# Whole 128 blocks in a padded MLP, and table work moved between engines, in a fused adaLN, long-convolution and MLP kernel

## The chip, the cores and the metric

The kernel runs on one core of a Trainium2 chip. The time is device microseconds of one execution; the number given for a kernel is the median of several executions. The engines of the core work side by side and meet through semaphores: PE (TensorE, matmuls; its weight loads are listed apart as PEld), DVE (VectorE), ACT (ScalarE), POOL (GpSimd) and SP (SyncE, which here only issues DMAs).

## The reference

A sequence of 2048 tokens of width 640 goes through a layernorm with scale and shift, a long convolution by FFT (a state-space mixer), a second modulated layernorm, and an MLP block. Cut to what matters:

```python
def _A_ref(q, k, v, shift_k, ssm_k, ssm_D):     # S = 2048, D = 640
    k_shift = sum of 4 shifted copies of k, each times a column of shift_k
    kv = k_shift * v
    y = irfft(rfft(pad(kv, 2*S)) * rfft(pad(ssm_k, 2*S)))[:S]
    return q * (y + kv * ssm_D)

def _B_ref(x, w1, w2, w3, w4):                  # F = 1728
    h = gelu(layernorm(x) @ w1)                 # 640 -> 640
    hs = (quarters of h, shifted by 1, -1, 2, -2 tokens) @ w2
    x1 = x + hs
    return x1 + gelu(layernorm(x1) @ w3) @ w4   # 640 -> 1728 -> 640

sa, ca, ga, sb, cb, gb = silu(c) @ w_mod
h = layernorm(x) * (1 + ca) + sa
x = x + ga * _A_ref(h, k, v, shift_k, ssm_k, ssm_D)
h = layernorm(x) * (1 + cb) + sb
out = x + gb * _B_ref(h, w1, w2, w3, w4)
```

All tensors are bf16. The inner width 1728 is 13 blocks of 128 and one of 64.

## The kernel before

**How work is ordered.** The kernel writes down tasks (`add(engine, cost, function, r=, w=, prio=)`), each with an engine, an estimated cost in us, the regions it reads and writes, and a priority (smaller goes first). A planner (`Planner.run`, L90) then simulates the five engines with these costs: an engine that comes free takes, among the tasks whose inputs are ready, the one with the smallest priority. The order that comes out is fixed: each engine executes its instructions strictly in that order, and semaphores make it wait where the data is not there. So a cost or a priority changed in one place can move instructions of other tasks, and an engine that stands at one instruction holds everything behind it in its queue.

**The convolution.** The FFT of length 4096 is done as two stages of matmuls against tables of sines and cosines, and its inverse likewise. The tables are made in the kernel at its start: POOL writes integer ramps (`iota`), DVE turns them into angles (`angles`, L316: a multiply-add at L323, a bitwise and for the modulus at L324), and ACT takes the sine (`sin_to`, L328; the instruction is at L331).

- `F1bd` is the block-diagonal table of stage 1: eight Sins of 32 rows by 32 columns into a zeroed tile (L284).
- `Gs` (in region RG) is the table of stage 2, in four blocks `kb`: from one ramp of 512 columns, eight DVE pairs and 16 Sins of 128x512, four of which write the same cosine a second time.
- `EA` and `EB` are small tables of the first inverse stage.
- `Hs` (in region RH) is the table of the last inverse stage, in four blocks `nb`: one ramp, eight DVE pairs, eight Sins of 128x512. Its integer scratch lies in region RK.

First the state-space kernel `ssm_k` is loaded (region Ra), turned by five DVE transposes (`to_slots`, L386, each after a one-column add, L442) and transformed (stage 1 at L399, stage 2 at L418, PSUM evacuated by ACT at L229 or DVE at L231). Meanwhile k is transposed on PE (L461), shifted by matmuls with diagonal weights (`diagw`, made by a POOL select at L350; L474) and multiplied with v on DVE (L480); the product goes through the same stages. The modulation vectors come from `w_mod` (loads at L497, matmuls at L507, called mod pieces here), which need the Silu of c at L378; that Silu stands behind the last Sin of the H table. The input x is loaded at L543 into region Ra when the second stage 1 has read it. The first inverse stage (`inverse1`: a DMA at L603 that swaps halves, two DVE products at L608 and L610, matmuls at L619 and L620) is followed by the last one (`inverse2`, L648).

**The MLP block.** Eight groups `g` of 256 tokens pass through DVE chains and layernorms, whose small statistics are computed on POOL (`ln_finish`, L685 to L694, and `ln1_fin`, L575 to L578). SP turns normalized tokens by DMA transposes (L734, called hT here, and L839). Then `mm_w1` (L764, L774), `mm_w2` (L819), `mm_w3` (L854, gelu at L859, L861 and L862) and `mm_w4` (L877). In `mm_w3` the stationary operand is a block of w3 (128 rows by 128 columns, the last one 64 columns) and 256 tokens move; five matmuls add up one block, 14 blocks make 70 matmuls a group. In `mm_w4` the stationary operand is a block of the gelu's output (128 features by 128 tokens, the last one 64 features) and 320 output columns move; 14 matmuls for each half of a tile of 128 tokens make 56 a group. w3 and w4 are loaded by SP (L900 to L902) over the region T01 once inverse2 has read it.

Of the kernel before, what the change touches and what calls it, by code (L numbers as in the profile page):

```python
# [8 lines left out]
BF = mybir.dt.bfloat16  # L9
F32 = mybir.dt.float32  # L10
# [6 lines left out]
P = 128  # L17
# [4 lines left out]
PI_LO = 3.1415925  # L22
LFFT = 4096
# [134 lines left out]
def kernel(  # L158
# [125 lines left out]
    add("POOL", 0.3, lambda e: nc.gpsimd.memset(F1bd[:], 0.0), w=[("F1", 0, 1)], prio=-2)  # L284
    add("POOL", 0.6, lambda e: make_identity(nc, ident), w=[("modB", 5, 6)], prio=5)

    def f(e):
        nc.vector.tensor_single_scalar(pci[:, 0:1], pidx[:], 31, ALU.bitwise_and)
        nc.vector.tensor_single_scalar(pci[:, 1:2], pidx[:], 63, ALU.bitwise_and)
        nc.vector.tensor_copy(s32[:], pci[:, 0:1])  # L290
        nc.vector.tensor_scalar(s32o[:], pci[:, 0:1], 2.0, 1.0, ALU.mult, ALU.add)
        nc.vector.tensor_copy(s64[:], pci[:, 1:2])
    add("DVE", 0.7, f, r=[("pidx", 0, 1)], w=[("scol", 0, 1)], prio=-2)

    gcol = mem.tile([P, 2, 4], F32, name="gcol")
    hcol = mem.tile([P, 2, 4], F32, name="hcol")
    ci = mem.tile([P, 4], I32, name="ci")

    def f(e):
        nc.gpsimd.iota(ci[:], pattern=[[16, 4]], base=0, channel_multiplier=0)  # L300
    add("POOL", 0.2, f, w=[("ci", 0, 1)], prio=-3)

    def f(e):
        for col, s_ in ((gcol, s64), (hcol, s32o)):
            nc.vector.tensor_scalar(col[:, 0, :], ci[:], s_[:], None, ALU.mult)
            nc.vector.tensor_scalar(col[:, 1, :], ci[:], s_[:], 2048.0, ALU.mult, ALU.add)
    add("DVE", 0.5, f, r=[("ci", 0, 1), ("scol", 0, 1)], w=[("cols", 0, 1)], prio=-1)
    tmp = {"R3": R3[:].bitcast(I32), "RK": RK[:].bitcast(I32)}

    def itab(reg, o, n, pattern, base, prio):  # L310
        ti = tmp[reg][:, o:o + n]
        add("POOL", 0.2 + 0.0012 * n, lambda e: nc.gpsimd.iota(ti, pattern=pattern, base=base, channel_multiplier=0),
            w=[(reg, 2 * o, 2 * o + 2 * n)], prio=prio)
        return ti, (reg, 2 * o, 2 * o + 2 * n)

    def angles(it, reg, o, s_col, cs_col, ss_col, q, prio):  # L316
        ti, tk = it
        n = ti.shape[1]
        ms, ma = (tmp[reg][:, o + n * i:o + n * (i + 1)] for i in range(2))
        keys = [(reg, 2 * o + 2 * n * i, 2 * o + 2 * n * (i + 1)) for i in range(2)]  # L320
        for m_, k_, col in ((ms, keys[0], ss_col), (ma, keys[1], cs_col)):
            def f(e, m_=m_, col=col):
                nc.vector.tensor_scalar(m_, ti, s_col, col, ALU.mult, ALU.add)  # L323
                nc.vector.tensor_single_scalar(m_, m_, q - 1, ALU.bitwise_and)  # L324
            add("DVE", 0.2 + 0.0013 * n, f, r=[tk, ("cols", 0, 1), ("scol", 0, 1)], w=[k_], prio=prio)
        return ms, ma, keys
# [6 lines left out]

    it = itab("R3", 4608, 32, [[2, 32]], 1, -2)
    ms, ma, ky = angles(it, "R3", 4640, s32[:], 32.0, 0.0, 128, -1)
    for q in range(4):
        sl = slice(32 * q, 32 * q + 32)
        sin_to(F1bd[sl, q, 0, :], ma[sl, :], 128, 32, ky[1], ("F1", 0, 1, "f"), -1)
        sin_to(F1bd[sl, q, 1, :], ms[sl, :], 128, 32, ky[0], ("F1", 0, 1, "f"), -1, True)
    it = itab("R3", 0, 512, [[2, 8], [128, 64]], 1, -1)  # L340
    for kb in range(4):
        ms, ma, ky = angles(it, "R3", 512 + 1024 * kb, s64[:], gcol[:, 1, kb:kb + 1], gcol[:, 0, kb:kb + 1], 8192, -1)
# [6 lines left out]
        sin_to(Gs[:, k2s, 1, 1, :], ma3, 8192, 512, ky[1], wk, 0)  # L349
# [5 lines left out]
    it = itab("RK", 1536, 64, [[1, 64]], 0, 8)  # L355
    ms, ma, ky = angles(it, "RK", 1600, s64[:], 16.0, 0.0, 64, 30)
# [11 lines left out]
    it = itab("RK", 0, 512, [[1, 16], [64, 32]], 0, 8)  # L368
    for nb in range(4):
        ms, ma, ky = angles(it, "RK", 512, s32o[:], hcol[:, 1, nb:nb + 1], hcol[:, 0, nb:nb + 1], 8192, 30)  # L370
        n1s = slice(16 * nb, 16 * nb + 16)
        wk = ("RH", 1024 * nb, 1024 * nb + 1024, "h")
        sin_to(Hs[:, n1s, 0, :], ma.rearrange("p (a b) -> p a b", a=16), 8192, 512, ky[1], wk, 30)
        sin_to(Hs[:, n1s, 1, :], ms.rearrange("p (a b) -> p a b", a=16), 8192, 512, ky[0], wk, 30, True)
# [285 lines left out]
    w3_sb = T0[:, 0:ND * F].rearrange("p (b n) -> p b n", b=ND)  # L660
# [180 lines left out]
    def mm_w3(g, prio):  # L841
        xT, xTk = xnT[g % 3]
        gk3 = ("R5", 10240 + 3584 * (g % 2), 10240 + 3584 * (g % 2) + 3584, ("g3", g))
        for f0 in range(0, NF, 4):
# [3 lines left out]
            def f(e, ps=ps, f0=f0, fn=fn):  # L848
                pt = pst(ps, [P, 4, 256], name="ps_w3")
                for fl in range(fn):  # L850
                    fb = f0 + fl
                    fw = min(P, F - fb * P)
                    for b in range(ND):
                        nc.tensor.matmul(pt[:fw, fl, :], lhsT=w3_sb[:, b, fb * P:fb * P + fw], rhs=xT[:, b, :], start=(b == 0), stop=(b == ND - 1))  # L854
# [114 lines left out]
```

## Time and profile before

| what | value |
|---|---|
| median of three runs | 369.92 us (368.13 to 370.08) |
| profiled execution | 368.94 us |
| its span, first to last instruction | 367.2 us |
| mean granted TensorE clock | 0.916 |
| PE busy | 290.1 us, 79% |
| PEld busy | 213.8 us, 58% |
| DVE busy | 234.7 us, 64% |
| ACT busy | 226.8 us, 62% |
| POOL busy | 80.1 us, 22% |

Busy time is the time in which an engine executes instructions; a share of the whole span hides that the stages have different limits, so stages are read one at a time. The chain of waits is followed back from the last instruction: at each step to what released it, or to the instruction before it on its engine. In the chain, "x56" means 56 instructions of one line in one piece. In a row of a timeline or a group, the line number is that of the kernel, what is written stands left of the arrow, and shapes are partitions by elements; for a matmul or a weight load, "64*128" are the active rows and columns of the array.

### The profile page before, as it was taken

Reading aid. Unit: us, or ns where it says so; the run is one execution under the profiler, and the core shown is the slowest. Engines: PE = TensorE matmul, PEld = TensorE weight load, DVE = VectorE, ACT = ScalarE, POOL = GpSimd, SP = SyncE. Lnnn points to the kernel's source line nnn. Section 1 sums busy time; section 2 is a strip of 40 time slices with the busy share of each in tenths; the row PEclk is TensorE's granted clock in tenths of the full one; section 3 lists DMA queues with packets and bytes.
Section 4 is the critical chain, followed back from the end, with each engine's and each line's share of the span. In section 5 each row is a group of like instructions: output and inputs, shape, how many; then the busy total and the mean of one; then the engine's idle time right before and its main releaser. Section 6 shows DMA issues by size and latency. Waiting matters only on the chain.

```text
span 367.2 us, 7656 instructions
## 1 busy us (share of the span) xinstructions
PE 290.1 (79%) x3086; PEld 213.8 (58%) x3092; DVE 234.7 (64%) x436; ACT 226.8 (62%) x362; POOL 80.1 (22%) x201
## 2 busy tenths in 40 slices
PE   0459789899834787501686999999999999999993
PEld 0336445577524776401554887786776776768672
DVE  8999999889089899988789786532313031211313
ACT  6959886679905588887789897693471412213020
POOL 8300000000020001485587573341130000000000
PEclk9989999999985799555868999999999999999997
DMA  7999404085962580079012505205010212101001
GB/s 217 339 199 234 142 0 116 2 266 108 215 206 67 133 203 4 4 290 267 3 36 54 91 15 108 61 0 83 26 38 20 54 29 45 38 10 29 18 21 36
DMA packets 49060, 35.08 MB, mean 96 GB/s; under 512 B 35008, under 2 KB 45952, under 8 KB 49024
## 3 DMA queue, kind: packets, MB, share of 16 engines
q1 hardware_dynamic: 47984, 30.39, 34.8%
q0 software_dynamic: 1040, 4.20, 3.4%
q8 instruction: 24, 0.39, 0.4%
q14 instruction: 12, 0.10, 0.1%
HBM read 18.85 MB, written 2.62 MB: 58 GB/s over the span
## 4 chain that ended last, share of the span: by engine, by line
PE 55%; DVE 25%; DMA 8%; ACT 4%; issue 3%; POOL 3%; SPq 1%; DVEq 0%; POOLq 0%; ACTq 0%
PE ps_w L877 18%; PE ps_w L854 18%; PE ps_w L819 6%; PE ps_w L764 5%; DMA Ra<-in_A_q_dram 4%; DVE ln_st L569 3%; DVE Rb L386 3%; DVE R L480 2%; DVE Rb L610 2%; DVE Ra L386 2%; ACT T L229 2%; PE ps_ksh L474 2%; DMA R<-RK 2%; PE ps_s L399 2%; DVE T L231 2%
## 5 line engine op out<-in xcount | busy, mean ns | idle before, releaser
L854 PE MATMUL ps_w<-R,T 128*128 128x256 bf16 (+1 forms) x560 | 66.3, 277 | 2.6 <-DMA R<-RH 2.6
L883 DVE TENSOR_TENSOR T<-ps_w,R 128x640 bf16<-128x640 f32 x16 | 13.2, 825 | 86.3 <-PE ps_w L877 86.3
L877 PE MATMUL ps_w<-T,R 128*128 128x320 bf16 x448 | 68.1, 300 | 0.0
L859 ACT ACTIVATE R<-ps_w 128x1024 bf16<-128x1024 f32 x24 | 24.5, 1022 | 61.7 <-PE ps_w L854 61.6
L854 PEld LDWEIGHTS <-T 128*128 128x128 bf16 (+1 forms) x560 | 54.5, 100 | 13.2 <-issue 6.0
L877 PEld LDWEIGHTS <-R 128*128 128x128 bf16 x448 | 41.7, 97 | 25.6 <-issue 8.4
L229 ACT CAST R<-ps_s 128x640 bf16<-128x640 f32 x49 | 31.4, 744 | 3.2 <-PE ps_s L418 3.2
L764 PE MATMUL ps_w<-R,RG 128*128 128x256 bf16 x160 | 20.4, 287 | 16.3 <-DMA R<-RK 16.3
L619 PE MATMUL ps_i<-EA,Rb 128*128 128x128 bf16 x160 | 23.2, 243 | 11.4 <-DVE Rb L608 11.4
L819 PE MATMUL ps_w<-RG,R 128*128 128x320 bf16 x160 | 25.7, 317 | 5.5 <-ACT R L780 4.1
L699 ACT ACTIVATE RG<-R 128x640 bf16<-128x640 bf16 x32 | 23.5, 736 | 9.9 <-DVE R L827 7.3
L229 ACT CAST T<-ps_s 128x1024 bf16<-128x1024 f32 x25 | 23.7, 1020 | 7.3 <-PE ps_s L399 7.3
L399 PE MATMUL ps_s<-F1bd,Rb 128*128 128x256 bf16 x80 | 13.3, 337 | 18.7 <-DVE Ra L442 14.3
L764 PEld LDWEIGHTS <-RG 128*128 128x128 bf16 x160 | 16.4, 103 | 19.7 <-issue 16.6
L418 PE MATMUL ps_s<-T,RG 64*128 64x160 bf16 x512 | 24.4, 230 | 2.8 <-ACT R L229 0.5
L620 PE MATMUL ps_i<-EB,Rb 128*128 128x128 bf16 x160 | 23.0, 243 | 3.7 <-DVE Rb L610 3.7
L229 ACT CAST T<-ps_i 128x1024 bf16<-128x1024 f32 x20 | 19.6, 1014 | 10.1 <-PE ps_i L620 6.5
L619 PEld LDWEIGHTS <-Rb 128*128 128x128 bf16 x160 | 17.8, 111 | 11.9 <-DVE Rb L608 11.9
L418 PEld LDWEIGHTS <-RG 64*128 64x128 bf16 x512 | 18.1, 94 | 10.9 <-issue 10.2
L819 PEld LDWEIGHTS <-R 128*128 128x128 bf16 x160 | 15.9, 103 | 13.6 <-ACT R L780 4.8
L399 PEld LDWEIGHTS <-Rb 128*128 128x128 bf16 x80 | 9.5, 120 | 22.2 <-DVE Ra L442 14.3
L620 PEld LDWEIGHTS <-Rb 128*128 128x128 bf16 x160 | 17.6, 111 | 5.0 <-DVE Rb L610 5.0
(123 smaller groups left out, 529.5 us busy)
## 6 DMA issues: line engine op xcount, KB each, us to landing
Rb<-in_w_mod_dram SPq DMA_DIRECT2D x6, 800.0 KB, 6.1
RK<-R SPq DMA_DIRECT2D x12, 256.0 KB, 3.8
R<-in_A_k_dram POOLq DMA_DIRECT2D x4, 640.0 KB, 13.5
Ra<-in_A_q_dram SPq DMA_DIRECT2D x4, 640.0 KB, 9.7
out_dram<-RH SPq DMA_DIRECT2D x64, 40.0 KB, 1.6
T<-in_B_w_dram SPq DMA_DIRECT2D x1, 2160.0 KB, 8.2
T<-in_B_w_dram SPq DMA_DIRECT2D x1, 2080.0 KB, 13.9
Rb<-R SPq DMA_DIRECT2D x8, 256.0 KB, 3.7
```

Of the source, the lines that this page charges most:

```text
L229: nc.scalar.copy(dst, src(ps.tile))
L386: add("DVE", 1.95, lambda e: nc.vector.transpose(out=o, in_=i), r=skeys, w=[(dkey, 2048 * b, 2048 * b + 2048)], prio=prio)
L399: nc.tensor.matmul(psv[:, ml, :], lhsT=xL[:, s0:s0 + P], rhs=F1r, start=True, stop=True)
L418: nc.tensor.matmul(psv[:, g, kl, :], lhsT=Gs[64 * g:64 * g + 64, k0 + kl, cc, :, :].rearrange("p o n -> p (o n)"), rhs=T1h[h][64 * g:64 * ...
L619: nc.tensor.matmul(psv[:, w, :], lhsT=TA[:, o:o + P], rhs=EAf, start=True, stop=False)
L620: nc.tensor.matmul(psv[:, w, :], lhsT=TB[:, o:o + P], rhs=EBf, start=False, stop=True)
L699: add("ACT", 0.83, lambda e: nc.scalar.activation(junk, src, ACT.Square, scale=float(D) ** -0.5, accum_out=stat[:, li, 1, t:t + 1]), r=[sk ...
L764: nc.tensor.matmul(pt[:, fb, :], lhsT=w1_sb[:, b, 160 * fb:160 * fb + P], rhs=hT[:, b, :], start=(b == 0), stop=(b == ND - 1))
L819: nc.tensor.matmul(pt[:, hf, 0:320], lhsT=gsf[:, fb, c0:c0 + P], rhs=w2_sb[:, fb, 320 * hf:320 * hf + 320], start=(fb == 0), stop=(fb == 4))
L854: nc.tensor.matmul(pt[:fw, fl, :], lhsT=w3_sb[:, b, fb * P:fb * P + fw], rhs=xT[:, b, :], start=(b == 0), stop=(b == ND - 1))
L859: nc.scalar.activation(g3[g % 2][:, f0:f0 + fn, :], ps.tile[:, 0:fn, :], ACT.Gelu_apprx_tanh)
L877: nc.tensor.matmul(pt[:, hf, 0:320], lhsT=g3[g % 2][:fw, fb, i * P:(i + 1) * P], rhs=w4_sb[:fw, fb, 320 * hf:320 * hf + 320], start=(fb == ...
```

## The change

There are three parts.

1. w3 in SBUF gets 1792 columns a row block in place of 1728, with zeros in the last 64, and the lower 64 rows of the last block of w4 are zeroed. All matmuls of `mm_w3` and `mm_w4` then use whole 128x128 blocks, and the last gelu is one instruction over two blocks. A new POOL task writes the zeros when inverse2 is done with the region, ahead of the loads. The planner's cost of `mm_w4` goes from 4.0 to 3.82.
2. The angles of the H table are computed on POOL, as fractions of a turn: a multiply-add, an add and subtract of a large constant that rounds to the nearest integer, and a subtraction. ACT takes the sine of 2 pi times the fraction. One buffer of angles serves all eight halves. Each block of G and H gets a ramp of its own, so the column helpers go; the scratch of the G angles is three sets, used in turn.
3. One of the four quarters of each G block, a cosine that is there twice, is copied by POOL. The first table is made by two Sins over 128 rows, and two POOL selects spread it over the block diagonal.

```diff
+    def angles(reg, o, n, pattern, base, s_col, q, prio):
+        ti, ms, ma = (tmp[reg][:, o + n * i:o + n * (i + 1)] for i in range(3))
...
+        add("POOL", 0.2 + 0.0012 * n, lambda e: nc.gpsimd.iota(ti, pattern=pattern, base=base, channel_multiplier=0),
+            w=[keys[0]], prio=prio)
+        for m_, k_, off in ((ms, keys[1], 0.0), (ma, keys[2], float(q // 4))):
+            def f(e, m_=m_, off=off):
+                nc.vector.tensor_scalar(m_, ti, s_col, off, ALU.mult, ALU.add)
+                nc.vector.tensor_single_scalar(m_, m_, q - 1, ALU.bitwise_and)
+            add("DVE", 0.13 + 0.0017 * n, f, r=[keys[0], ("scol", 0, 1)], w=[k_], prio=prio)
+
+    def angles_pool(reg, o, n, pattern, base, s_col, prio):
...
+        for off in (0.0, 0.25):
+            def f(e, off=off):
+                nc.gpsimd.tensor_scalar(xs, ti, s_col, off, ALU.mult, ALU.add)
+                nc.gpsimd.tensor_scalar(xr, xs, MAGIC, MAGIC, ALU.add, ALU.subtract)
+                nc.gpsimd.tensor_tensor(xs, xs, xr, ALU.subtract)
+            add("POOL", 0.6 + 0.0036 * n, f, r=[keys[0], ("scol", 0, 1)], w=keys[1:], prio=prio)
+            yield xs, keys[1]
+
+    def turns_to(dst, xs, n, r, w, prio, neg=False):
+        sc = (-2.0 if neg else 2.0) * PI_LO
+        add("ACT", 0.2 + 0.00098 * n, lambda e: nc.scalar.activation(dst, xs, ACT.Sin, scale=sc), r=[r], w=[w], prio=prio)
...
-    for q in range(4):
-        sl = slice(32 * q, 32 * q + 32)
-        sin_to(F1bd[sl, q, 0, :], ma[sl, :], 128, 32, ky[1], ("F1", 0, 1, "f"), -1)
-        sin_to(F1bd[sl, q, 1, :], ms[sl, :], 128, 32, ky[0], ("F1", 0, 1, "f"), -1, True)
-    it = itab("R3", 0, 512, [[2, 8], [128, 64]], 1, -1)
+    sin_to(F1c[:, 0, :], ma, 128, 32, ky[1], ("F1c", 0, 1, "f"), -1)
+    sin_to(F1c[:, 1, :], ms, 128, 32, ky[0], ("F1c", 0, 1, "f"), -1, True)
+        nc.gpsimd.affine_select(out=F1v, in_=src, pattern=[[-32, 4], [0, 64]], compare_op=ALU.is_ge, fill=0.0, base=0, channel_multiplier=1)
+        nc.gpsimd.affine_select(out=F1v, in_=F1v, pattern=[[32, 4], [0, 64]], compare_op=ALU.is_ge, fill=0.0, base=31, channel_multiplier=-1)
+    add("POOL", 0.8, f, r=[("F1c", 0, 1)], w=[("F1", 0, 1)], prio=-1)
     for kb in range(4):
-        ms, ma, ky = angles(it, "R3", 512 + 1024 * kb, s64[:], gcol[:, 1, kb:kb + 1], gcol[:, 0, kb:kb + 1], 8192, -1)
+        ms, ma, ky = angles("R3", 1536 * (kb % 3), 512, [[2, 8], [128, 64]], 1 + 16 * kb, s64[:], 8192, 1)
...
-        sin_to(Gs[:, k2s, 1, 1, :], ma3, 8192, 512, ky[1], wk, 0)
+        add("POOL", 0.75, lambda e, k2s=k2s: nc.gpsimd.tensor_copy(Gs[:, k2s, 1, 1, :], Gs[:, k2s, 0, 0, :]), r=[wk[:3]], w=[wk], prio=4)
...
-    it = itab("RK", 0, 512, [[1, 16], [64, 32]], 0, 8)
     for nb in range(4):
-        ms, ma, ky = angles(it, "RK", 512, s32o[:], hcol[:, 1, nb:nb + 1], hcol[:, 0, nb:nb + 1], 8192, 30)
-        sin_to(Hs[:, n1s, 0, :], ma.rearrange("p (a b) -> p a b", a=16), 8192, 512, ky[1], wk, 30)
-        sin_to(Hs[:, n1s, 1, :], ms.rearrange("p (a b) -> p a b", a=16), 8192, 512, ky[0], wk, 30, True)
+        for i, (xs, xk) in enumerate(angles_pool("RK", 0, 512, [[1, 16], [64, 32]], 16 * nb, s32o[:], 8)):
+            turns_to(Hs[:, n1s, 1 - i, :], xs.rearrange("p (a b) -> p a b", a=16), 512, xk, wk, 30, neg=(i == 0))
...
-    w3_sb = T0[:, 0:ND * F].rearrange("p (b n) -> p b n", b=ND)
+    FP = NF * P
+    w3_sb = T0[:, 0:ND * FP].rearrange("p (b n) -> p b n", b=ND)
...
-                        nc.tensor.matmul(pt[:fw, fl, :], lhsT=w3_sb[:, b, fb * P:fb * P + fw], rhs=xT[:, b, :], start=(b == 0), stop=(b == ND - 1))
+                        nc.tensor.matmul(pt[:, fl, :], lhsT=w3_sb[:, b, fb * P:(fb + 1) * P], rhs=xT[:, b, :], start=(b == 0), stop=(b == ND - 1))
...
-                if f0 + fn < NF:
-                    nc.scalar.activation(g3[g % 2][:, f0:f0 + fn, :], ps.tile[:, 0:fn, :], ACT.Gelu_apprx_tanh)
-                else:
-                    nc.scalar.activation(g3[g % 2][:, f0:f0 + fn - 1, :], ps.tile[:, 0:fn - 1, :], ACT.Gelu_apprx_tanh)
-                    nc.scalar.activation(g3[g % 2][0:64, NF - 1, :], ps.tile[0:64, fn - 1, :], ACT.Gelu_apprx_tanh)
+                nc.scalar.activation(g3[g % 2][:, f0:f0 + fn, :], ps.tile[:, 0:fn, :], ACT.Gelu_apprx_tanh)
...
-                        fw = min(P, F - fb * P)
-                        nc.tensor.matmul(pt[:, hf, 0:320], lhsT=g3[g % 2][:fw, fb, i * P:(i + 1) * P], rhs=w4_sb[:fw, fb, 320 * hf:320 * hf + 320],
+                        nc.tensor.matmul(pt[:, hf, 0:320], lhsT=g3[g % 2][:, fb, i * P:(i + 1) * P], rhs=w4_sb[:, fb, 320 * hf:320 * hf + 320],
...
-            t0 = add("PE", 4.0, f, r=[gk3, ("T01", 10240, 10240 + NF * D)], alloc=ps, prio=prio)
+            t0 = add("PE", 3.82, f, r=[gk3, ("T01", 10240, 10240 + NF * D)], alloc=ps, prio=prio)
...
+        nc.gpsimd.memset(w3_sb[:, :, F:FP], 0.0)
+        nc.gpsimd.memset(w4_sb[64:128, NF - 1, :], 0.0)
+    add("POOL", 1.2, f, w=[("T01", 0, ND * FP), ("T01", 10240, 10240 + NF * D)], prio=101)
```

## The prediction

> **What bounds the kernel now.** I read four views: busy time by stage, the chain of waits, the timelines of the first 100 us, the groups by shape. Stages first (busy us and count of each engine in each stretch, then clock and DMA):
>
> ```profile
> core 0: us, PE busy (x) PEld busy (x) DVE busy (x) ACT busy (x) POOL busy (x), PEclk, DMA share, GB/s
> 0.00:35.00 35.00, 16.03 (x123) 11.72 (x125) 32.24 (x58) 27.69 (x41) 10.95 (x22) 0.95 0.95 241
> 35.00:62.00 27.00, 23.52 (x245) 13.53 (x248) 25.28 (x41) 20.98 (x32) 0.00 (x0) 1.00 0.31 94
> 62.00:87.00 25.00, 23.03 (x268) 16.56 (x266) 22.36 (x23) 20.05 (x27) 0.00 (x0) 1.00 0.40 119
> ...
> 150.00:199.00 49.00, 22.26 (x355) 15.28 (x336) 42.16 (x101) 41.57 (x80) 33.13 (x75) 0.67 0.42 119
> 199.00:260.00 61.00, 60.73 (x475) 46.44 (x476) 36.60 (x85) 44.48 (x88) 26.39 (x68) 0.97 0.33 58
> 260.00:362.00 102.00, 101.42 (x780) 73.44 (x778) 23.78 (x42) 30.05 (x46) 4.45 (x18) 1.00 0.13 30
> ```
>
> PE is busy for 60.73 of 61 us and 101.42 of 102 us: from 199.27 to 361.45 the kernel is bound by PE alone, and a nanosecond taken off a matmul there is taken off the end. Before that no engine rules: in 0 to 35 it is DVE (32.24), in 35 to 87 DVE, PE and ACT are all 78 to 94% busy, and in 150 to 199 PE is mostly idle while small steps on POOL, DVE and SP follow one another.
>
> The chain of waits (start, length, what) prices the matmuls. Two clean groups first, all of 128x128 weights:
>
> ```profile
> 216.59 2.18 PE ps_w L764 x20
> ...
> 243.02 2.72 PE ps_w L819 x20
> ```
>
> 256 moving columns cost 2.18/20 = 0.109 us each, 320 columns 2.72/20 = 0.136. Now the two products of the last MLP, which have a partial block (1728 = 13 x 128 + 64):
>
> ```profile
> 330.98 7.97 PE ps_w L854 x70
> 338.95 8.34 PE ps_w L877 x56
> ```
>
> At the clean prices 56 of L877 would take 56 x 0.136 = 7.62 us and 70 of L854 70 x 0.109 = 7.63: 0.72 and 0.34 us are extra in each of the eight groups. The timeline of weight loads shows where:
>
> ```profile
> 289.75 1.70 PEld L877 LDWEIGHTS <-R 128*128 128x128 bf16 x13
> 291.71 1.85 PEld L877 LDWEIGHTS <-R 64*128 64x128 bf16 x14 [0.26 <-issue]
> 293.83 1.85 PEld L877 LDWEIGHTS <-R 64*128 64x128 bf16 x14 [0.26 <-issue]
> ```
>
> After 13 full loads the 64-row load starts 0.26 us late. Matmul starts, read one by one, agree: 0.232 us before a 64-row matmul and 0.239 after it in place of 0.136, and 0.011 on the next; around the five 64-column matmuls of L854 0.203, 0.134 and 0.205 in place of 0.109, and 0.011.
>
> [...] 0.09 to 0.10 us at each change to or from a 64-row or 64-column block. [...] DVE, then POOL:
>
> ```profile
> 14.17 0.12 DVE L442 TENSOR_TENSOR Ra<-Ra,Dcol 128x1 bf16<-128x1 bf16 x1
> ...
> 16.34 0.91 DVE L442 TENSOR_TENSOR Ra<-Ra,Dcol 128x1 bf16<-128x1 bf16 x1
> ```
>
> ```profile
> 14.77 2.47 POOL L350 TENSOR_SCALAR_AFFINE_SELECT RQ<-skT 128x2560 bf16<-128x2560 bf16 x1 [6.17 <-DMA skT<-in_A_shift_k_dram]
> ```
>
> The same one-column add takes 0.12 us alone and 0.91 when it meets the POOL select, ending as that ends. [...]
>
> **The change, part by part.**
>
> *Padding (L854, L861, L862, L877).* No matmul and no moving column is added or removed. In each half tile of L877 the extra was 96 + 103 + 11 = 210 ns; 32 halves give 6.7 us. In each L854 group 94 + 25 + 96 + 11 = 226 ns; 8 give 1.8. Sum 8.5 us, on the PE-bound stretch. About 2.2 groups of eight lie before 260, where hT transposes come 2 to 9 us ahead of their w1 matmuls, so little of that can turn into waiting: I take -8.0 (0 if the extra has another cause, -8.5 at most). Joining L861 and L862 (382 + 366 ns) saves ACT about 0.15 us a group; ACT is 30 of 102 us busy there: nothing.
>
> *The two memsets on POOL.* They wait for the last inverse2 matmul (156.7), and the w3/w4 loads, issued at 156.80, may wait for them. The weights land at 165 to 171 and are first used at 199: their delay is covered by 28 us. Not covered: POOL is on the chain of waits from 150.91 to 166.4 with the layernorm steps, queued behind the memsets, and the first hT transpose (166.48, 6.43 us) lands just after the w4 load does. By the rows of 5 columns (0.12 us) and 256 (0.30) I estimate 0.4 + 0.6 = 1.0 us. Low end 0 (POOL idles 0.9 us before 156.66), high end +3 (placed too early, POOL stands until 156.7). I take +1.0.
>
> *First table and its block diagonal.* Eight 32-row Sins (0.31 us) become two plus two POOL selects, and four column helpers leave DVE (0.5 us). The selects wait for the table load and the Sins (about 4.1 us), and what POOL issues after them, one sT load and the k loads, goes out some 2 us later; k is first used at 32 and landed by 22, so that costs nothing; the last sT block (landed 14.49) is then turned third or fourth of five. Between 0 and nothing.
>
> *G table.* Its angles now rank behind to_slots, and its iotas on POOL behind the DMA issues. DVE no longer fills 3 to 12 us with angles, but begins the 2.07 us transposes as blocks land (5.43, 6.94, 10.08, 12.24, 14.49): they end near 18.5 in place of 23.5, and the angles (8 pairs, 0.57 + 0.34 us apart: 7.3, up to 9 where POOL meets them) follow among the evacuations. ACT loses four of 16 Sins and the small ones: 2.6 + 1.8 us. Remaining at 16: 12 evacuations of 1.05, 7.8 of Sins on ACT, 8 to 9 of angles on DVE: shared out, both end at about 32 to 32.5 in place of 33.5. I take -1.0; -3 with good packing, +3 where the five adds (up to 0.8 each) and the angles meet POOL.
>
> *H table.*
>
> ```profile
> L331 ACT ACTIVATE RG<-R,b_pos 128x512 bf16<-128x512 int32 x12 | 7.8, 712 | 0.0
> ...
> L323 DVE TENSOR_SCALAR RK<-RK,s32o,hcol 128x512 int32<-128x512 int32 x8 | 4.3, 539 | 0.0
> ...
> L324 DVE TENSOR_SCALAR RK<-RK 128x512 int32<-128x512 int32 x8 | 3.4, 427 | 0.3
> ```
>
> Sixteen DVE instructions leave the stretch 35 to 62: starts 0.57 + 0.34 apart, 8 x 0.91 = 7.3 us of 25.28. ACT's eight Sins stay. PE has only 3.5 us idle there and 2 in the next stretch, so it is late next; evacuations go to DVE. [...] One buffer serves all eight, so each round is group + half an iota (0.3) + Sin (0.72) + two hand-overs (0.3) = 3.9; from 33 us 31 us, to 64; the Silu behind the last Sin and its copy (1.28 + 0.21 + 0.81) end at 66.5, ahead of the first mod piece (71.44). Queued on ACT behind a Sin that waits are evacuations; behind the RK tables SP's RK loads (57.36), which have 50 us to spare, and after them the second w_mod loads (73.0). I take -1.5 (PE's idle time bounds it at -5; +4 by stalls on ACT). What is gained here passes on: x loads start when the kv stage1 ends (85.67) and DVE waits for them to 101.99.
>
> Sum: -8.0 + 1.0 - 1.0 - 1.5 = -9.5. From 368.94 (span 367.2 and 1.74 around it) that is 359.4; the profiled execution lies 1.0 below the median, 369.92, so 360.4; I say 360.5.
>
> **Rivals.**
> - *The front gives back* (POOL meets DVE, ACT waits for angles, the memset comes at a bad place: +4): the fixed order of each queue speaks for it, the free time of ACT against it. 369.9 - 8 + 3 = 365.
> - *The front pays in full*: DVE is on the chain for most of 28 to 70; PE's idle time is against it. -8.5 - 6 = 355.5.
> - *The padding buys nothing*, the extra being of the operands and not of the block: against it the clean L819, same columns. 369.9 - 2 = 368.
> - *The other side*: the H table as the new bound. If a POOL group takes over 4.7 us (1.57 an operation), a round is 6, eight end at 81, and Silu, mod pieces and loads move 11 us; that eats the gain. It decides from there; at 5.2 it gives 373. Against it: [...]the rows of 0.6 to 0.72 us.
>
> **Numbers.** Likeliest 0.55 (360.5, own range 357 to 364), 365: 0.20, 355.5: 0.12, 368: 0.05, 373: 0.08. The range 354.5 to 367 leaves out the last two and a rest. No change is within 0.5%, 368.1 to 371.8, about what the three runs (368.13 to 370.08) can tell. Faster 0.55 + 0.20 + 0.12 and half of the fourth = 0.89, less 0.02 for its edges: 0.87; same 0.05; slower 0.08.
>
> **What would show it.** L854 x70 at 7.63 and L877 x56 at 7.62 in the chain, no load late by 0.2; w3 starting before 199; to_slots done near 18.5 with angles behind; POOL groups of 2.6 us and the Silu before 67; memsets near 157. Wrong: the extra staying at another block, PE idle after 199, or mod pieces waiting for Silu.

## The result, and the profile after

| what | before | after |
|---|---|---|
| median, both measured together | 369.24 us (368.13 to 370.08) | 372.77 us (372.08 to 373.95, four runs) |
| ratio | 1 | 1.0101 (95%: 1.0059 to 1.0143) |
| profiled execution, span | 368.94, 367.2 us | 372.08, 370.3 us |
| last ssm_k transpose of `to_slots` ends | 23.60 | 18.61 |
| stage 1 of ssm_k ends | 32.00 | 34.06 |
| last Sin of the H table ends | 58.42 | 71.76 |
| Silu starts | 50.94 | 75.99 |
| first mod piece | 71.44 | 81.87 |
| stage 1 of kv ends (x loads are issued) | 85.64 | 96.36 |
| first `inverse1` matmul | 114.55 | 125.10 |
| first `mm_w1` | 173.01 | 182.55 |
| first `mm_w3` | 199.27 | 209.14 |
| last `mm_w4` ends | 361.42 | 364.51 |

The changed kernel is slower by about 1%. One row needs a word: the Silu is made to follow the Sin of the H table that is written down last, which need not be the one that runs last. In the kernel before one Sin still ran after it (timeline of ACT, before; in brackets the idle time before a row and who ended it):

```profile
50.94 0.21 ACT L378 ACTIVATE silu_c<-c_col 128x5 f32<-128x5 bf16 x1
...
57.70 0.72 ACT L331 ACTIVATE RH<-RK,b_pos 128x512 bf16<-128x512 int32 x1 [0.86 <-DVE RK L324]
```

Read down the table, the slowdown is two large amounts of opposite sign. At the end of stage 1 of kv it is 10.7 us behind, and still 9.9 us behind at the first `mm_w3`; from there to the last `mm_w4` it makes up 6.8 us (162.15 against 155.37 us).

The part that makes up time first. The chain of waits of the kernel after (start, length, what; L857 was L854, L875 was L877), then the timeline of its weight loads:

```profile
336.20 7.64 PE ps_w L857 x70
343.84 7.61 PE ps_w L875 x56
```

```profile
328.32 7.54 PEld L875 LDWEIGHTS <-R 128*128 128x128 bf16 x56
```

A group of 70 now takes 7.64 us and one of 56 takes 7.61, the clean prices of the prediction to 0.01 us, and 56 loads stand in one piece where the kernel before broke after 13 and 14 with a load 0.26 us late. Where the blocks no longer change, the 0.34 and 0.72 us of extra a group are gone.

Now the part that loses it. Busy time by stage, columns as before:

```profile
core 0: us, PE busy (x) PEld busy (x) DVE busy (x) ACT busy (x) POOL busy (x), PEclk, DMA share, GB/s
...
35.00:62.00 27.00, 22.49 (x228) 12.99 (x231) 17.62 (x23) 15.50 (x26) 21.15 (x18) 0.94 0.10 31
62.00:87.00 25.00, 20.71 (x204) 12.97 (x205) 17.48 (x18) 14.37 (x23) 7.78 (x6) 0.86 0.27 72
...
199.00:260.00 61.00, 55.09 (x435) 42.35 (x434) 43.98 (x105) 54.34 (x107) 32.62 (x92) 0.97 0.30 55
260.00:362.00 102.00, 102.00 (x841) 82.11 (x840) 24.92 (x44) 30.39 (x37) 3.44 (x12) 1.00 0.14 33
```

In 35 to 62 DVE falls from 25.28 to 17.62 us, as meant, and POOL takes 21.15. But ACT, whose eight Sins the change leaves to it, falls from 20.98 to 15.50, and PE from 23.52 to 22.49; in 62 to 87 PE falls from 23.03 to 20.71. All three wait for something. What DVE still does there takes it as long as before (35 to 87 us: 1.22 us for a product L483 and 0.82 for an evacuation of 640 columns, with 1.21 and 0.81 before), so meetings with POOL are not it. The waits between 30 and 100 us say what is (engine, what it does, what it waited for: us in all, times, the longest); the kernel before, then the kernel after:

```profile
ACT RH L331 <- DVE RK L324: 1.5, 2, 0.9
```

```profile
ACT RH L328 <- POOL RK L322: 17.4, 7, 3.2
DVE R L483 <- PE ps_ksh L477: 13.0, 7, 3.4
...
PE ps_ksh L477 <- ACT R L230: 5.3, 3, 2.7
```

In the kernel before, ACT waited for the H angles 1.5 us in all, two times. Here it is 17.4 us in seven, one for each half of the table but the first. The other two lines are what stands behind ACT: matmuls of the k shift waiting for ACT to empty a buffer of PSUM, where matmuls write, and DVE waiting for those matmuls. The granted clock in these two stretches is 0.94 and 0.86, where it was 1.00; what share of the loss that is, no run separates. The timeline of ACT, after, shows the order in its queue (start, busy, line and operation):

```profile
42.00 0.63 ACT L328 ACTIVATE RH<-RK 128x512 bf16<-128x512 f32 x1 [1.64 <-POOL RK L322]
42.54 1.27 ACT L230 CAST R<-ps_s 128x640 bf16<-128x640 f32 x2
43.71 1.01 ACT L230 COPY R<-ps_kT 128x1024 bf16<-128x1024 bf16 x1
46.89 0.63 ACT L328 ACTIVATE RH<-RK 128x512 bf16<-128x512 f32 x1 [2.17 <-POOL RK L322]
47.42 1.28 ACT L230 CAST R<-ps_s 128x640 bf16<-128x640 f32 x2
51.72 0.63 ACT L328 ACTIVATE RH<-RK 128x512 bf16<-128x512 f32 x1 [3.01 <-POOL RK L322]
...
74.70 1.28 ACT L381 ACT_TABLE_LOAD   x1
75.99 0.21 ACT L381 ACTIVATE silu_c<-c_col 128x5 f32<-128x5 bf16 x1
```

Each of the Sins (L328) that wait has 1 to 3 us of PSUM evacuations (L230) queued behind it, and each stands for 1.6 to 3.2 us. The timeline of POOL over one round shows what it waits for:

```profile
42.80 0.70 POOL L320 TENSOR_SCALAR RK<-RK,s32o 128x512 f32<-128x512 int32 x1 [0.28 <-ACT RH L328]
43.59 1.92 POOL L321 TENSOR_SCALAR RK<-RK 128x512 f32<-128x512 f32 x1
45.59 1.26 POOL L322 TENSOR_TENSOR RK<-RK 128x512 f32<-128x512 f32 x1
47.61 0.70 POOL L320 TENSOR_SCALAR RK<-RK,s32o 128x512 f32<-128x512 int32 x1 [0.76 <-ACT RH L328]
```

The three operations take 0.70, 1.92 and 1.26 us; with the gaps between them the group is 4.1 us (42.80 to 46.85), where the prediction had 2.6 and the planner's cost for it is 2.44. Sins start 4.85 us apart (42.00 to 71.13, six rounds), not 3.9. The Silu, last behind them, runs at 75.99, and its copy on DVE and the first mod piece come at 81.00 and 81.87; the prediction had the Silu and its copy done at 66.5. In this kernel, though, the mod pieces hardly wait for the Silu: PE is busy from 76.78 up to the first of them, and its wait for the copy is 0.2 us. They are late because the work ahead of them in PE's order is.

Two smaller items. The memsets (timeline of POOL, before and after), and the wait ahead of the first `mm_w1` (timeline of PE, before and after):

```profile
156.66 0.32 POOL L692 TENSOR_TENSOR ln_rs<-stat,ln_m 128x2 f32<-128x2 f32 x1 [0.91 <-ACT RG L699]
```

```profile
164.97 0.36 POOL L899 MEMSET T<- 128x320 bf16 x1
165.39 0.63 POOL L900 MEMSET T<- 64x640 bf16 x1
```

```profile
173.01 3.61 PE L764 MATMUL ps_w<-R,RG 128*128 128x256 bf16 x20 [16.28 <-DMA R<-RK]
```

```profile
182.55 4.43 PE L768 MATMUL ps_w<-R,RG 128*128 128x256 bf16 x20 [16.28 <-DMA R<-RK]
```

They take 0.36 and 0.63 us, the 0.4 and 0.6 of the prediction. They run just ahead of the layernorm step for which POOL stood idle 0.91 us before, and fill that gap. They start 1.3 us before the last `inverse2` matmul ends (166.27): by the offsets in the code, the columns that they zero are last read by the group of tiles before it. PE's wait before `mm_w1` is 16.28 us in both kernels, so nothing of the memsets can be seen on the path.

The G table: stage 1 of ssm_k ends 2 us later although its transposes end 5 us earlier. DVE, ACT and PE, after:

```profile
12.88 1.37 DVE L445 TENSOR_TENSOR Ra<-Ra,Dcol 128x1 bf16<-128x1 bf16 x1
...
18.49 0.94 DVE L305 TENSOR_SCALAR R<-R,s 128x512 int32<-128x512 int32 x1
...
19.80 0.48 DVE L305 TENSOR_SCALAR R<-R,s 128x512 int32<-128x512 int32 x1
...
27.87 3.48 DVE L232 CAST T<-ps_s 128x1024 bf16<-128x1024 f32 x3
```

```profile
8.93 9.35 ACT L230 CAST T<-ps_s 128x1024 bf16<-128x1024 f32 x10 [6.13 <-PE ps_s L402]
19.92 0.72 ACT L333 ACTIVATE RG<-R,b_neg 128x512 bf16<-128x512 int32 x1 [1.64 <-DVE R L306]
...
27.21 1.33 ACT L333 ACTIVATE RG<-R,b_pos 128x512 bf16<-128x512 int32 x2
28.45 0.99 ACT L230 CAST T<-ps_s 128x1024 bf16<-128x1024 f32 x1
```

```profile
18.33 0.60 PE L402 MATMUL ps_s<-F1bd,Rb 128*128 128x256 bf16 x4 [0.32 <-ACT T L230]
29.14 4.91 PE L402 MATMUL ps_s<-F1bd,Rb 128*128 128x256 bf16 x24 [10.21 <-DVE T L232]
```

The transposes end at 18.6. Then the angles fill DVE until 27.9 and the Sins fill ACT until 28.5, both ahead of the evacuations, and PE, its PSUM buffers full, stands 10.21 us. In the kernel before the same work had been done while blocks were still loading, and PE was busy for 5.16 of the 9.5 us from 18.5 to 28; here for 0.43. Meetings with POOL are there as well: the one-column add that takes 0.16 us elsewhere takes 1.37, ending as the POOL select does (14.25 and 14.24), and three of the eight angle multiplies take 0.83 to 0.94 in place of 0.48, each beside a POOL instruction (17.87 to 19.14, 20.36 to 21.23 and 21.57 to 22.44).

### The profile page after: what moved, and what is told of

Its sections match the earlier page's. It is cut to its first block, busy times and chain, and to the rows that moved or that the text cites. A ratio compares the mean times of both kernels' runs of the same rounds, so it can differ in the third digit from the quotient of the medians.

```text
span 370.3 us, 7656 instructions
## 1 busy us (share of the span) xinstructions
PE 286.1 (77%) x3086; PEld 217.2 (59%) x3092; DVE 228.4 (62%) x418; ACT 221.6 (60%) x343; POOL 114.7 (31%) x237
## 3 DMA queue, kind: packets, MB, share of 16 engines
q1 hardware_dynamic: 47984, 30.39, 33.5%
## 4 chain that ended last, share of the span: by engine, by line
PE 38%; DVE 23%; POOL 13%; ACT 12%; DMA 7%; issue 6%; SPq 0%; POOLq 0%; DVEq 0%; ACTq 0%
PE ps_w L875 14%; PE ps_w L857 14%; DMA Ra<-in_A_q_dram 4%; PE ps_w L823 4%; POOL RK L321 4%; DVE ln_st L572 3%; ACT RG L703 3%; POOL RK L322 2%; DVE Rb L389 2%; POOL ln_rs L697 2%; ACT T L230 2%; DVE Rb L613 2%; DVE R L727 2%; DMA Ra<-in_A_ssm_k_dram 2%; ACT R L784 2%
## 5 line engine op out<-in xcount | busy, mean ns | idle before, releaser
L861 ACT ACTIVATE R<-ps_w 128x1024 bf16<-128x1024 f32 (+1 forms) x32 | 29.2, 916 | 65.8 <-PE ps_w L857 65.3
L857 PE MATMUL ps_w<-R,T 128*128 128x256 bf16 x560 | 62.9, 273 | 1.2 <-DMA R<-RH 0.9
L875 PE MATMUL ps_w<-T,R 128*128 128x320 bf16 x448 | 62.3, 299 | 0.0
L857 PEld LDWEIGHTS <-T 128*128 128x128 bf16 x560 | 54.7, 98 | 8.3 <-issue 1.6
L875 PEld LDWEIGHTS <-R 128*128 128x128 bf16 x448 | 43.8, 98 | 16.5
L768 PE MATMUL ps_w<-R,RG 128*128 128x256 bf16 x160 | 20.9, 290 | 16.3 <-DMA R<-RK 16.3
L230 ACT CAST T<-ps_s 128x1024 bf16<-128x1024 f32 x27 | 25.7, 1023 | 11.0 <-PE ps_s L402 10.9
L230 ACT CAST R<-ps_s 128x640 bf16<-128x640 f32 x48 | 30.6, 734 | 2.7 <-PE ps_s L421 2.6
L622 PE MATMUL ps_i<-EA,Rb 128*128 128x128 bf16 x160 | 20.5, 227 | 11.5 <-DVE Rb L611 11.5
L421 PEld LDWEIGHTS <-RG 64*128 64x128 bf16 x512 | 20.2, 100 | 12.2 <-issue 11.6
L823 PEld LDWEIGHTS <-R 128*128 128x128 bf16 x160 | 16.2, 105 | 17.9 <-ACT R L770 5.6
L477 PE MATMUL ps_ksh<-R,RQ 128*128 128x512 bf16 x74 | 21.0, 411 | 6.3 <-ACT R L230 5.3
L230 ACT CAST T<-ps_i 128x1024 bf16<-128x1024 f32 x20 | 19.2, 1016 | 9.1 <-PE ps_i L623 5.2
L402 PEld LDWEIGHTS <-Rb 128*128 128x128 bf16 x80 | 10.1, 127 | 23.7 <-issue 12.7
L622 PEld LDWEIGHTS <-Rb 128*128 128x128 bf16 x160 | 16.4, 102 | 12.2 <-DVE Rb L611 12.2
L623 PE MATMUL ps_i<-EB,Rb 128*128 128x128 bf16 x160 | 20.2, 227 | 4.2 <-DVE Rb L613 4.2
## 6 DMA issues: line engine op xcount, KB each, us to landing
R<-in_A_k_dram POOLq DMA_DIRECT2D x4, 640.0 KB, 10.1
```

What stands on the lines that cost most here:

```text
L230: nc.scalar.copy(dst, src(ps.tile))
L402: nc.tensor.matmul(psv[:, ml, :], lhsT=xL[:, s0:s0 + P], rhs=F1r, start=True, stop=True)
L421: nc.tensor.matmul(psv[:, g, kl, :], lhsT=Gs[64 * g:64 * g + 64, k0 + kl, cc, :, :].rearrange("p o n -> p (o n)"), rhs=T1h[h][64 * g:64 * ...
L477: nc.tensor.matmul(pt[:, i, :], lhsT=diagw[:, b, jj, :], rhs=kT[:, b, 16 - jj + sc * 512:16 - jj + sc * 512 + 512], start=(jj == 0), stop= ...
L622: nc.tensor.matmul(psv[:, w, :], lhsT=TA[:, o:o + P], rhs=EAf, start=True, stop=False)
L623: nc.tensor.matmul(psv[:, w, :], lhsT=TB[:, o:o + P], rhs=EBf, start=False, stop=True)
```

## The experiments

Each kernel was timed beside the kernel before on the same chip; the runs are from three chips, on which the median of the kernel before was 369.18 to 369.98. My theory after the result: a POOL group dearer than both the prediction and the planner had it makes ACT stand at its Sins with evacuations behind them; the planner's cost, not POOL's time alone, puts the Sins where they stand. The rivals: POOL's serial rounds delay the Silu and by it the mod pieces; the G and first-table part is what costs; the padding does not bring what its groups show.

| run | median us | ratio (95%) | kv stage 1 ends |
|---|---|---|---|
| e1 padding alone | 361.95 | 0.9801 (0.9748 to 0.9853) | 85.39 |
| e11 the same again | 363.14 | 0.9830 (0.9800 to 0.9861) | 86.46 |
| e8 padding, one G quarter copied on POOL | 362.64 | 0.9820 (0.9795 to 0.9844) | 85.92 |
| e12 after without padding | 380.07 | 1.0290 (1.0251 to 1.0330) | 96.07 |
| e2 after with H angles on DVE | 364.18 | 0.9853 (0.9793 to 0.9913) | 87.78 |
| e4 after, rounding in two single steps | 383.05 | 1.0356 (1.0297 to 1.0414) | 104.01 |
| e5 after, rounding in two multiply-adds | 367.81 | 0.9958 (0.9934 to 0.9982) | 91.39 |
| e3 after, POOL group at its measured cost | 369.10 | 1.0001 (0.9969 to 1.0033) | 88.93 |
| e6 e3 and the Silu early | 364.08 | 0.9855 (0.9827 to 0.9883) | 87.99 |
| e7 e3 and two angle buffers | 364.01 | 0.9857 (0.9814 to 0.9899) | 87.50 |
| e9 after with all four remedies | 362.40 | 0.9802 (0.9764 to 0.9840) | 85.33 |
| e10 padding and only the mended H table | 362.20 | 0.9785 (0.9751 to 0.9818) | 84.50 |

A median stands on several executions, a date in a trace on one. The traces of e1 and e11, the same kernel twice, differ by 1.1 us at the end of stage 1 of kv and by 4.9 at the first `mm_w3` (197.22 and 202.16), so dates that differ by less prove little.

### Which part costs: one part alone, or one undone

*e1_pad_only.* The kernel before with the first part of the change only.

```diff
+                        nc.tensor.matmul(pt[:, fl, :], lhsT=w3_sb[:, b, fb * P:(fb + 1) * P], rhs=xT[:, b, :], start=(b == 0), stop=(b == ND - 1))
...
+        nc.gpsimd.memset(w3_sb[:, :, F:FP], 0.0)
+        nc.gpsimd.memset(w4_sb[64:128, NF - 1, :], 0.0)
```

> The kernel before with the padding alone (zero columns and rows, the two memsets, one gelu over two blocks, planner cost 3.82). Theory A, that the padding gives its 8.5 us on the PE-bound stretch and the loss lies elsewhere: 360 to 362 us, L877's 56 matmuls in 7.61 us. Rival, that what PE saves is spent again as waiting for the layernorm chain before 260 us, as 3.2 us of PE idle time in the changed kernel suggest: 364 to 366. If the memsets disturb POOL and SP: first w1 matmul later than 174 us.

361.95, 7.6 us under the 369.53 of the kernel before beside it (e11: 6.8 under). The stretch from the first `mm_w3` to the last `mm_w4` is 155.56 us, 6.6 less than before, and PE is idle there for 1.5 us, where before it was not; together 8.0, most of the 8.5 of the block changes. That the front suffers can't be seen: the first `mm_w1` is at 171.33 here and at 175.56 in e11, with 173.01 before. The padding brings what its groups show.

*e12_front_only.* The changed kernel with the MLP of before.

```diff
-                        nc.tensor.matmul(pt[:, fl, :], lhsT=w3_sb[:, b, fb * P:(fb + 1) * P], rhs=xT[:, b, :], start=(b == 0), stop=(b == ND - 1))
+                        nc.tensor.matmul(pt[:fw, fl, :], lhsT=w3_sb[:, b, fb * P:fb * P + fw], rhs=xT[:, b, :], start=(b == 0), stop=(b == ND - 1))
```

> The changed kernel without the padding: both table parts, and the MLP as before. If the two parts of the change add up (padding -7.6 as measured alone, changed kernel +3.5 in all), the table parts alone cost about 11 us: 380 to 382. If the padding is worth less in the changed kernel, where PE waits 3.2 us after its first w3 matmul: 377 to 379.

380.07, 10.1 us above the 369.98 beside it. The two halves add up: -7.6 + 10.1 = +2.5, and the whole change measured +3.5 (372.77 - 369.24), a difference that medians good to about 1 us don't resolve.

*e2_h_on_dve.* The changed kernel, but with the H angles on DVE.

```diff
-        for i, (xs, xk) in enumerate(angles_pool("RK", 0, 512, [[1, 16], [64, 32]], 16 * nb, s32o[:], 8)):
-            turns_to(Hs[:, n1s, 1 - i, :], xs.rearrange("p (a b) -> p a b", a=16), 512, xk, wk, 30, neg=(i == 0))
+        ms, ma, ky = angles("RK", 0, 512, [[1, 16], [64, 32]], 16 * nb, s32o[:], 8192, 30)
+        sin_to(Hs[:, n1s, 0, :], ma.rearrange("p (a b) -> p a b", a=16), 8192, 512, ky[1], wk, 30)
+        sin_to(Hs[:, n1s, 1, :], ms.rearrange("p (a b) -> p a b", a=16), 8192, 512, ky[0], wk, 30, True)
```

> The changed kernel with the angles of the H table back on DVE (a ramp for each block, the rest of the change kept). Theory A, that the POOL angles cost all of the front's loss: kv stage 1 ends at 84 to 87 us and the time is 359 to 362. Rival B, that the G table's new order or the POOL copies carry a good part: kv stage 1 ends after 90 and the time is above 365.

364.18, between the two expectations: undoing this one item takes 8.6 us off, so the H table on POOL is nearly the whole loss. What is left against padding alone (361.95 and 363.14) is 1.0 to 2.2 us for the first table and G, with intervals that overlap. That stage 1 of ssm_k ends later by them is shown: at 33.5 to 34.2 in the nine traces in which the angles follow `to_slots`, at 31.8 to 32.8 in the five in which they lead. That this costs anything at the end is not.

*e8_pad_copy.* Padding, and of the G part only the copy of one quarter by POOL.

```diff
-        sin_to(Gs[:, k2s, 1, 1, :], ma3, 8192, 512, ky[1], wk, 0)
+        add("POOL", 0.75, lambda e, k2s=k2s: nc.gpsimd.tensor_copy(Gs[:, k2s, 1, 1, :], Gs[:, k2s, 0, 0, :]), r=[wk[:3]], w=[wk], prio=4)
```

> The padding, and of the table part only the quarter of each G block copied by POOL; G's angles stay ahead of to_slots, H stays on DVE. If the 2.2 us by which the kernel with H on DVE lags behind the padding alone come from the G angles placed behind to_slots: 360 to 362.5 here, the last to_slots at 23.3 to 24.5 and stage 1 of ssm_k done by 32. If the POOL copies themselves cost (they meet DVE's one-column adds and angles): 363 to 366.

362.64, just above its first expectation and not distinguishable from padding alone. `to_slots` ends at 25.64 in place of 23.30 (e1) and 23.49 (e11), but stage 1 at 32.58, with 31.76 and 32.81 there. So the copy is not what is left of e2's gap beyond 0.7 us; the new place of the angles, shown above, is the likelier cause of the later stage 1, but no run tried it alone.

### How it costs: POOL's time, the planner's cost, the Silu

*e4_split and e5_multadd.* The rounding step of the changed kernel (L321) written in two other ways, with the planner's cost left as it is.

```diff
-                nc.gpsimd.tensor_scalar(xr, xs, MAGIC, MAGIC, ALU.add, ALU.subtract)
+                nc.gpsimd.tensor_scalar(xr, xs, MAGIC, None, ALU.add)
+                nc.gpsimd.tensor_scalar(xr, xr, MAGIC, None, ALU.subtract)
```

> The changed kernel with the add and subtract of the large constant (1.93 us) as two POOL instructions of one operation each. If the cost is that of the form with two constants, each part takes about 0.7 us, a round is 0.5 us shorter, eight rounds 4 us, and the time is about 369. If it is the operation on fp32 itself, the parts take about 1 us each and the time stays at 372 to 374.

383.05, beyond every expectation. The timeline of POOL in e4_split shows why:

```profile
43.97 0.69 POOL L320 TENSOR_SCALAR RK<-RK,s32o 128x512 f32<-128x512 int32 x1 [0.28 <-ACT RH L329]
44.75 1.50 POOL L321 TENSOR_SCALAR RK<-RK 128x512 f32<-128x512 f32 x1
46.33 1.50 POOL L322 TENSOR_SCALAR RK<-RK 128x512 f32<-128x512 f32 x1
47.91 1.27 POOL L323 TENSOR_TENSOR RK<-RK 128x512 f32<-128x512 f32 x1
```

Each single step takes 1.50 us, so the group grows from 4.1 to about 5.2 us and rounds from 4.85 to 6.0. ACT waits for POOL 25.4 us in place of 17.4.

```diff
-                nc.gpsimd.tensor_scalar(xr, xs, MAGIC, MAGIC, ALU.add, ALU.subtract)
+                nc.gpsimd.tensor_scalar(xr, xs, 1.0, MAGIC, ALU.mult, ALU.add)
+                nc.gpsimd.tensor_scalar(xr, xr, 1.0, -MAGIC, ALU.mult, ALU.add)
```

> The changed kernel with the rounding step (1.93 us) as two POOL instructions, each a multiply by 1 and an add, the form of the first instruction of the group, which takes 0.70 us. If POOL is quick in this form, each part takes about 0.7 us, a round falls by 0.5 us and the time to about 368. If what makes the first one quick is its int32 input or its column operand, each part stays at 1.5 to 1.9 us, a round grows by 1.2 to 1.9 us and the time is 382 to 388.

The timeline of POOL in e5_multadd:

```profile
41.98 0.69 POOL L320 TENSOR_SCALAR RK<-RK,s32o 128x512 f32<-128x512 int32 x1 [0.29 <-ACT RH L329]
42.75 0.62 POOL L321 TENSOR_SCALAR RK<-RK 128x512 f32<-128x512 f32 x1
43.45 0.62 POOL L322 TENSOR_SCALAR RK<-RK 128x512 f32<-128x512 f32 x1
44.15 1.26 POOL L323 TENSOR_TENSOR RK<-RK 128x512 f32<-128x512 f32 x1
```

Two multiply-adds of the same tile take 0.62 us each and together less than the one add-and-subtract of 1.92. The group is 3.4 us, rounds are 4.25, ACT waits 12.5 us, and the kernel takes 367.81. With the changed kernel between them, three points lie near one line: rounds of 4.25, 4.85 and 6.0 us give 367.8, 372.8 and 383.1, so 8.3 and 9.0 us for each us of a round. There are eight halves, so in this order of instructions the serial rounds are paid nearly in full.

*e3_pool_cost.* No instruction changes; only the planner is told 4.2 us for a group.

```diff
-            add("POOL", 0.6 + 0.0036 * n, f, r=[keys[0], ("scol", 0, 1)], w=keys[1:], prio=prio)
+            add("POOL", 4.2, f, r=[keys[0], ("scol", 0, 1)], w=keys[1:], prio=prio)
```

> The changed kernel with only the planner's cost of one POOL angle group raised from 2.44 to 4.2 us, near the 4.1 measured; the same instructions in another order. Theory A1, that the loss is ACT standing in its fixed order at Sins planned too early (17.4 us in seven waits): the waits of ACT for POOL fall below 5 us in all and the time is 361 to 366, although eight rounds on POOL still take 39 us. Rival A2, that the serial rounds themselves delay Silu and the mod pieces and so the rest: mod pieces start no earlier than 80 and the time stays above 369.

369.10. The groups are as long as before, but the waits of e3_pool_cost between 30 and 100 us have, in place of 17.4 us:

```profile
ACT RH L328 <- POOL RK L322: 1.7, 2, 1.3
```

Stage 1 of kv ends at 88.93 in place of 96.36. So most of the 10.7 us at that point came from the fixed order, made with a cost of 2.44, in which ACT reached each Sin too early. But of the 7.4 us only 3.7 arrive at the end: the first expectation was right about the waits and wrong about the time, the second right about the time. The timeline of ACT in e3_pool_cost shows what is late next:

```profile
77.16 0.66 ACT L328 ACTIVATE RH<-RK 128x512 bf16<-128x512 f32 x1
77.84 1.28 ACT L381 ACT_TABLE_LOAD   x1
79.13 0.21 ACT L381 ACTIVATE silu_c<-c_col 128x5 f32<-128x5 bf16 x1
```

The last Sin starts at 77.16 and the Silu behind it at 79.13; the mod pieces begin at 81.64, and the loads of `w_mod` that wait for them are issued at 83.19, only 5.8 us before the x loads (12.7 in the kernel before). DVE begins on x at 107.53, 18.6 us after the x loads are issued, where it was 16.3: the x loads take 13.0 us from issue to landing in place of 9.7 (medians), and the DMA engines, idle in the kernel before from 85.5 to 87, are over 80% busy from 88 on, before the x loads are issued. That the late `w_mod` loads are the cause is an inference from this; no run tried it. The first `inverse1` is at 120.08, 31.2 us after the end of stage 1 of kv; in the kernel before it was 28.9.

*e6_silu_early and e7_two_buffers.* Two ways to take this away, both on top of e3: the Silu no longer behind the last Sin, or a second buffer, so that POOL doesn't wait for ACT.

```diff
-    sl_t = add("ACT", 1.6, lambda e: nc.scalar.activation(silu_c[:], c_col[:], ACT.Silu), r=[("ccol", 0, 1)], w=[("siluc", 0, 1)], prio=35, after=[last_sin])
+    sl_t = add("ACT", 1.6, lambda e: nc.scalar.activation(silu_c[:], c_col[:], ACT.Silu), r=[("ccol", 0, 1)], w=[("siluc", 0, 1)], prio=25)
```

> The kernel with the planner's POOL cost at 4.2, and the Silu no longer made to follow the last Sin of the H table. If what is left of the loss there (369.1 against 364.2 with H on DVE) is the Silu behind eight serial POOL rounds, which delays mod pieces, the second w_mod loads and with them the x loads: mod pieces start at 71 to 76, the first inverse1 matmul comes at 116 to 118 and the time is 363 to 366. If it is the other order of the evacuations: mod pieces early, but the time stays at 368 to 370.

364.08. The Silu goes first (timeline of ACT in e6_silu_early):

```profile
36.52 1.28 ACT L381 ACT_TABLE_LOAD   x1
37.81 0.21 ACT L381 ACTIVATE silu_c<-c_col 128x5 f32<-128x5 bf16 x1
40.50 0.63 ACT L328 ACTIVATE RH<-RK 128x512 bf16<-128x512 f32 x1
```

The table of H is done later than in any other run (last Sin at 81.79), and it costs nothing: `inverse2`, which reads it, starts at 146. So the date of the H table itself doesn't matter; what stood behind it in ACT's queue did. Of the 5.0 us gained over e3, 2.6 are there at the first `inverse1`. The rest lies between there and `mm_w3`, which I did not take apart; e1 and e11, the same kernel, differ by 2.8 us in that stretch.

```diff
+            xs, kx = ((tmpf[reg][:, o + n:o + 2 * n], keys[1]), (tmpf[reg][:, 1536:2048], (reg, 3072, 4096)))[j]
...
-            add("POOL", 0.6 + 0.0036 * n, f, r=[keys[0], ("scol", 0, 1)], w=keys[1:], prio=prio)
-            yield xs, keys[1]
+            add("POOL", 4.2, f, r=[keys[0], ("scol", 0, 1)], w=[kx, keys[2]], prio=prio)
+            yield xs, kx
```

> The kernel with the planner's POOL cost at 4.2, and a second buffer for the angles, so that POOL can compute the next half while ACT takes the Sin of one. If the single buffer makes the rounds serial: rounds fall from 5.0 to about 4.4 us, the last Sin ends at about 70 in place of 77.8, Silu and mod pieces come 7 us earlier, and the time is 364 to 367. If POOL's own speed is all of it: last Sin after 75 and the time at 368 to 370.

364.01, by the other way: rounds fall from 5.7 to 4.4 us because POOL works on while ACT takes the sine, the Silu starts at 72.78 and the mod pieces at 77.04. Both agree with e2 (364.18). With the right price and one more remedy, POOL's table is as good as DVE's, and not better.

### Whether a mended version beats padding alone

*e9_mended* is the changed kernel with the multiply-adds, the cost of 3.5, two buffers and the early Silu. *e10_pad_pool_mended* is padding with that H table, and F1 and G as before. *e11_pad_again* repeats padding alone beside them.

> The changed kernel with all that the runs showed put right, angles still on POOL: rounding as two multiply-adds (group about 3.5 us, planner cost 3.5), two angle buffers, Silu ahead of the H Sins. If POOL takes 7.3 us of angles off DVE for something once it no longer holds up ACT: below 361. If PE is late next there, and the G table's place costs its 1 to 2 us: 361.5 to 364.5, no better than the padding alone.

> The padding with the mended POOL angles of the H table, and the first table and the G table as in the kernel before. If DVE was the bound of 35 to 62 us, kv stage 1 ends 2 to 4 us earlier than with the padding alone (85.4) and the time is 358 to 360. If PE and ACT are late next: 85 to 86 and 361 to 363.

> The kernel with the padding alone once more, on the same chip as the two mended ones: 361 to 363.

362.40, 362.20 and 363.14, with intervals that overlap: all three beat the kernel before by some 2%, and I can't tell them apart. e9 and e10 differ in the first table and the G table alone, so that part costs 0.2 us here, which is nothing that can be measured. The windows of e1_pad_only and of e10_pad_pool_mended suggest why taking work from DVE brings so little:

```profile
35.00:62.00 27.00, 23.50 (x248) 13.55 (x251) 25.27 (x41) 20.85 (x33) 0.00 (x0) 1.00 0.24 68
```

```profile
35.00:62.00 27.00, 25.06 (x278) 14.72 (x277) 21.51 (x27) 19.25 (x31) 17.20 (x23) 1.00 0.20 69
```

Against padding alone DVE is busy 3.8 us less in this stretch, and PE is now busy for 25.06 of 27 us in place of 23.50. PE has little left to give; that it is late next is read from this and not shown by a run of its own. At the end of stage 1 of kv this is worth 0.9 to 2.0 us (84.50 against 85.39 and 86.46), and at the end nothing that can be measured.

## Why the prediction was wrong

The prediction said 360.5 and faster; the result is 372.77 and slower by 1%. By its own steps:

- *Padding, -8.0.* Right: -7.6 and -6.8 alone (e1, e11), at the block changes where the extra was read, and the groups are at 7.61 and 7.64. The 0.5 held back for waiting was too little: PE is idle for 1.5 us behind the first `mm_w3` in e1 and for 2.4 in e11.
- *Memsets, +1.0.* Their durations were right, and nothing is seen of them at the end: the wait ahead of `mm_w1` is 16.28 us with and without them. The cover I found missing was there. They did not wait for the last `inverse2` matmul and fell into the 0.91 us in which POOL idled, which I had as the low end.
- *First table and G, -1.0.* `to_slots` ends at 18.61 as predicted (18.5). What went otherwise is the next thing, that the remaining evacuations, Sins and angles would be "shared out" and end at 32 to 32.5. They came one after the other, tables first, PE stood 10.21 us, and stage 1 ended at 34.06. Up to the end of this stage the gain of 1 us became a loss of about 2. At the end of the kernel the runs give a loss of 0.2 (e9 less e10) to 2.2 us (e2 less e1), not clear of noise, and no gain.
- *H table, -1.5.* This is the step that failed: +8.6 (after less e2). Two things were wrong in it. The first is a size, 2.6 us for a POOL group. The first two operations were priced at 0.7 each, by the select (2.47 us for 2560 columns) and the copy of 640 columns (0.72). The rest, for the third, was my estimate, shown by no trace: in the kernel before no `tensor_tensor` of POOL has more than 6 columns. The outer two measured 0.70 and 1.26. The middle one, add and subtract in one instruction, measured 1.92 and not 0.7; the trace of before has no row of that form either. Together that is 4.1 us in place of 2.6. The second is the mechanism. I looked for the turning point only at the end of the rounds, in the Silu, and so put it at a group of 4.7 us. Evacuations queued "on ACT behind a Sin that waits" were named, but priced at +4 at most, and left out of the likeliest sum. Nor does the sum ask where the planner, with a cost of 2.44 for a group, would put the Sins. Both decide well below 4.7: with groups of 3.4 us ACT still waits 12.5 us in all and the kernel is only 0.4% faster than before (e5), with padding in it.
- *The rivals.* The first, "the front gives back", named ACT waiting for angles among its causes and put the front at +4; that cause came, and the front cost 10.1 (e12). The other side, the H table as the new bound at 373, is where the time came out, but not by its path: its point of 4.7 us was not reached, and in the changed kernel the Silu's delay is not what is paid first. e3 shows both in turn: priced right, the waits on ACT go and the front gains 7.4 us; then the Silu's delay is the main part of what remains, and e6 removes it. "The padding buys nothing" is refuted by e1.
- *The sum.* -7.6 (e1), +1.0 to +2.2 (first table and G), +8.6 (H table) give +2.0 to +3.2; measured +3.5. These are differences of one chain of kernels, so that they add up says little. The check of its own is e12: the front alone costs 10.1, and -7.6 + 10.1 gives +2.5.

## What to carry to other kernels

A static order of instructions is made of cost estimates, and an estimate too low costs as a slow instruction does: ACT, put at a Sin 1.6 to 3.2 us too early seven times, held up matmuls through PSUM. Correcting one number with no instruction changed gave 3.7 us back (e3); a faster instruction with the number left wrong gave 5.0 (e5). When work moves to an engine for which the trace has no row of just that form, let the range reach to several times the nearest row (here 1.92 us where 0.7 was taken), and ask of every round what is queued behind the waiting engine before asking when the last round ends. And in a stage where three engines are 78 to 94% busy, ask what the second of them leaves: here the best H table took 3.8 us off DVE and 1 to 2 us off the stage.

## What the runs showed of the hardware

- On POOL, for 128x512 fp32 to fp32, the price of a `tensor_scalar` depends on its operations: (multiply, add) 0.61 to 0.65 us (e5, e9, e10), a single add or subtract 1.49 to 1.54 (e4), (add, subtract) 1.92 to 1.98 (after, e3, e7). From int32, with a column as multiplier, (multiply, add) is 0.70. 1.92 us for 512 columns is 3.8 ns a column, three times the multiply-add. Why the forms differ stays open.
- In e6 the Sins after the Silu's table load (1.28 us) ran with no second load: up to 200 us three table loads stand in that trace, as in the one of the changed kernel. In the kernel before, too, a Sin (57.70) followed the Silu (50.94) with no load between them. So the Silu could go first for nothing, and the trace of before already had the sign of it.
